# A gated recurrence with a soft mixture of experts: chunks of four units, one exponential for two units, and engine orders written out as lists

## The chip, the cores and the metric

The kernel runs on one core of one Trainium2 chip. The metric is the time on the device in microseconds, as the median of several runs. TensorE is called PE, VectorE DVE, ScalarE ACT, GpSimd POOL, and SyncE, whose queue issues the loads and stores, SP.

## The reference, cut to what matters

x, r_gate and i_gate are 4 x 5056 x 256 (batch, time, channels), in fp32; the output is 20224 x 256.

```
log_a   = 8 * sigmoid(r_gate) * log(clip(sigmoid(a_param)))
a_t     = exp(log_a);  norm = sqrt(max(1 - a_t*a_t, 1e-6))
h       = a_t * h + norm * sigmoid(i_gate) * x     # over time, for each batch
x       = h of all steps, as 20224 rows            # the y of the names below
logits  = x @ phi                                  # 32 slots
d       = softmax of logits over all 20224 rows
slot_in = d.T @ x                                  # 32 x 256, 4 slots for each of 8 experts
out_e   = max(slot_in[e] @ w1[e], 0) @ w2[e]       # 256 -> 1024 -> 256
output  = (softmax of logits over the 32 slots) @ out
```

The softmax over all rows ties the whole input together: no output row is known before the last step of the recurrence is done.

## The kernel before, in words

**Tiles.** The rows are cut into 40 blocks q of 512 (the last has 256). Two blocks make a unit p: unit 0 is q 0, units 1 to 19 are pairs, and unit 20 is q 39. The recurrence runs along the free dimension with channels on the partitions, in two halves h of 128 channels, so everything that comes in with rows on the partitions is transposed by PE.

**Steps of a unit, by their names.** A number behind a name is q, or p.h, or the group.
- Dr, Di, Dx: SP loads r, i and x, 512 KB each.
- TR (line 605): PE transposes r into a "pair" of PSUM banks. SR (616): ACT writes tanh(r/2) from there into slot A.
- EX (680): ACT takes the exponential of A in place, with a scale and a bias per channel; this is a_t. Before, each unit and half has its own.
- SQ (667): POOL squares A into slot N. RT (697): ACT takes the square root of 1 - N for both halves in one instruction.
- SI (629 sigmoid, 631 tanh): ACT makes the input gate for both blocks of a unit at once. A string IV says how, one letter for a unit: S is a sigmoid; P is a tanh with a step of POOL behind it (642); E is a tanh whose 1 is put right by PE, which transposes both i*x and x into the same bank.
- U (651): POOL multiplies gate and x. TU (716): PE transposes the product into a pair. ST (733): DVE multiplies it by the norm. SC (750): DVE scans it and overwrites A with the states.
- TY (774) and YC (790 on DVE, 788 on ACT): the states go back to rows on partitions, through a PSUM bank into a y tile "yn". Either engine can copy.
- For a group g of four blocks: LG (830) logits, LE (843) their running maximum, LD and TE the difference and its transpose, ES (884) and DM (891) two exponentials on ACT, AC (904) the sum over rows on PE, AE (920) its accumulation on DVE.
- CT (1270), CM (1281), CS (1284), CE (1287), RR (1291 to 1293), CN, CH, CL: the softmax over the slots.

Behind the last scan come a short chain (MT, MX, MR, MC, WJ, WE, W, SP), the experts' matmuls L1.0 to L1.7 (1153) and L2.0 to L2.7 (1201) with the weights w1 and w2 (named w10 to w17 and w20 to w27), and the output: HP (1335), HE (1346), OT (1358), OE (1370 on ACT, 1372 on DVE), and OD, the store (1382).

**Chunks.** ACT holds one set of function tables at a time: exp with tanh, sigmoid with tanh, or sqrt. A function of another set brings an ACT_TABLE_LOAD. So the units are cut into chunks, and for a chunk ACT does all SR and EX, then all SI, then all RT:

```
CHUNKS = [2, 2, 2, 2, 2, 2, 2, 2, 2, 2, 1]
IV = 'PPEESSSSSSSSSSSSSSSSP'
```

**Slots.** The data of A, N, x and i lie in 16 slots "b" of 8 KB per partition (two halves of eight 16 KB tiles); r lies in 7 tiles "st" of 4 KB, y in 8 tiles "yn". PSUM has three pairs and two single banks; of the pairs, TR may hold two, TU two and TY one. The weights and the output later use the b and st slots.

**Order.** A planner (class Planner, from line 111) builds the program: each step is a task with an assumed duration, its dependences, a priority and the slots that it takes, and `run` (line 153) starts on each engine the ready task of the best priority, as a list scheduler does. The order in which the tasks start becomes the fixed order of each engine's instructions. SP's loads stand in one queue, each of which waits for its slot, with all behind it. While PE would be idle early on, fillers (1030) keep it at work.

Of the kernel before, what the change touches and what calls it, by code (L numbers as in the profile page):

```python
# [17 lines left out]
J = 4  # L18
# [4 lines left out]
CHUNKS = [2, 2, 2, 2, 2, 2, 2, 2, 2, 2, 1]  # L23
# [5 lines left out]
IV = 'PPEESSSSSSSSSSSSSSSSP'  # L29
# [34 lines left out]
LATE = False  # L64
# [59 lines left out]
class Planner:  # L124
    def __init__(self, slots):
        self.tasks = []
        self.slots = {t: list(range(n)) for t, n in slots.items()}
        self.act_seq = []

        self.pair_max = {}  # L130
        self.pairs_of = {}

        self.pair_left = -1

        self.warm, self.warm_from, self.warm_to = None, 0.0, 0.0
# [14 lines left out]
    def run(self):  # L150
# [11 lines left out]
        self.table = "exp" if GATES0 else "ln"  # L162
# [55 lines left out]
        while n_done < len(self.tasks):  # L218
# [17 lines left out]
            while again:  # L236
                again = False
                for e in ("DVE", "ACT", "PE", "POOL", "SP"):
# [42 lines left out]
    def tag_for(self, b, taken={}):  # L281
        for g in b.tags:
            if b.kept is not None:
                return g
            if b.late is not None and not b.late(self, g):
# [7 lines left out]
        return None  # L293

# [74 lines left out]
def kernel(  # L369
# [122 lines left out]
    def e_const():  # L492
        nc.scalar.preload_act_table_set("exp_and_others" if GATES0 else "natural_log_exp_and_others")
# [8 lines left out]
    t_const = add("POOL", "const", 2.0, prio=-100, emit=e_const)  # L502
# [31 lines left out]
    def load(nm, q):  # L534
# [19 lines left out]
        ld[(nm, q)] = add("SP", f"D{nm}{q}", SPR * n / J + (1.2 if (nm, q) == ("x", PHI) else 0), prio=q, emit=emit, alloc=[] if own else [b], uses=[b] if own else [])  # L554
# [40 lines left out]
    def mk_sr(q):  # L595
# [15 lines left out]
        tr = add("PE", f"TR{q}", 0.25 * n, deps=[ld[("r", q)], t_const], prio=q - TRP, emit=e_tr,  # L611
                 alloc=[rp], uses=[st[("r", q)]], shape="T")

        def e_sr():
            dst = t(A[p])[:, :, i * QT : i * QT + c]
            nc.scalar.activation(dst, t(rp)[:, :, :c], AF.Tanh, scale=0.5)  # L616
# [57 lines left out]
    def mk_exh(p, h):  # L674
# [3 lines left out]
        def e_ex(h=h):  # L678
            v = T["b2"][A[p].slot[0] // 2][:, h::2, :] if len(us) == 2 else t(A[p])[:, h, :c]
            nc.scalar.activation(  # L680
                v, v, AF.Exp, scale=ca[:, h : h + 1], bias=ca[:, h : h + 1]
            )

        EX[(p, h)] = add("ACT", f"EX{p}.{h}", 0.29 + 0.853 * c / 1024 * len(us),
# [3 lines left out]
    def mk_rt(p):  # L688
        c = plen(p)
        wide = p in WIDE  # L690
        for h in range(1 if wide else H):
# [7 lines left out]
            RT[(p, h)] = add("ACT", f"RT{p}.{h}", 0.11 + 0.835 * c / 1024 * (H if wide else 1),  # L699
# [59 lines left out]
    def mk_y(q):  # L759
# [3 lines left out]
        for b0 in range(0, qlen(q) // P, step):  # L763
# [16 lines left out]
            ty = add("PE", f"TY{q}.{b0}", 0.24 * nb, deps=[SC[(p, h)] for h in range(H)],  # L780
# [21 lines left out]

    def exp_phase(pl):
        if pl.act_at >= len(pl.act_seq):
            return True
        return pl.table == "exp" and pl.act_seq[pl.act_at].kind == "exp"

    def mk_group(g):
# [63 lines left out]
        def e_te():  # L872
            for b in range(nb):
# [12 lines left out]
        ES[g] = add("ACT", f"ES{g}", 0.07 + 0.43 * nb * rows / QT, deps=[te], prio=pos - 30, emit=e_es,  # L886
# [38 lines left out]
        AE[g] = add("DVE", f"AE{g}", 0.42, deps=[ac] + ([DM[g], AE[g - 1]] if g else []), prio=pos - 30 + fin,  # L925
# [8 lines left out]
    def e_sa():  # L934
        if GATES0:
# [41 lines left out]
    for k in range(NC):  # L977
# [13 lines left out]
        if not k and not GATES0:  # L991
# [41 lines left out]
    planner.warm, planner.warm_from, planner.warm_to = e_warm, 4.0, WARMT  # L1033
# [10 lines left out]
    def late(pl, tag):  # L1044

        if tag == "st":
            return st[("i", NQ - 1)].tag is not None and len(pl.slots["st"]) >= 2
        return len(pl.slots["b"]) > sum(b.tag is None for b in [*A.values(), *Nb.values(), *xb.values(), *(ib[p] for p in ib if two_i(p)), *lSb, hz] if b.kept is None)
# [24 lines left out]
    sT.late = lambda pl, tag: yn[NQ - 1].tag is not None  # L1073
# [164 lines left out]

    planner.warm_late = lambda pl: LATE and SC[(NP - 1, 0)].start is not None and t_bd[0].start is None


    def quiet(pl):

        return SC[(NP - 3, H - 1)].start is None or l1s[0].start is not None

    def early(pl):
        return SC[(NP - 4, H - 1)].start is None or l1s[0].start is not None

    def late_hl(pl):
        return YC[NQ - 1][-1].end is not None and pl.now >= YC[NQ - 1][-1].end  # L1250
# [3 lines left out]
    def mk_c(g, first):  # L1254
# [7 lines left out]
        hl.late = lambda pl, tag: tag == "yn" and late_hl(pl) or tag != "yn" and l1s[-1].start is not None  # L1262
# [9 lines left out]
        k = add("PE", f"CT{g}", 0.12 * nb, deps=[LE[g]], prio=pc, gate=early, emit=e_ct, alloc=[cp], uses=[lSb[g // 4]], shape="T")  # L1272
# [13 lines left out]
        e = add("ACT", f"CE{g}", 0.12 + 0.43 * nb * rows / QT, deps=[k], prio=pr, kind="exp", gate=lambda pl: pl.act_at >= len(pl.act_seq),  # L1286
# [8 lines left out]
        r = add("DVE", f"RR{g}", 0.7 + 0.5 * nb * rows / QT, deps=[e], prio=pr + 0.2, emit=e_rr, gate=quiet, uses=[lSb[g // 4]])  # L1295
# [4 lines left out]
        k = add("POOL", f"CN{g}", 0.15 + 1.1 * nb * rows / QT, deps=[r], prio=pr, uses=[lSb[g // 4]],  # L1300
# [6 lines left out]
        k = add("POOL", f"CL{g}", 1.0, deps=[k], prio=pr, uses=[hl, lSb[g // 4]],  # L1307
# [9 lines left out]
    for i, g in enumerate(corder):  # L1317
# [6 lines left out]
        for og in ogs:  # L1324
            og.late = lambda pl, tag: l1s[-1].start is not None
        done = {j: [] for j in range(n)}
        for a0 in range(0, m, 8):
# [12 lines left out]
            k = add("PE", f"HP{g}.{a0}", 0.11 * aw / 2, deps=[t_hl], prio=pr - 6, gate=lambda pl: l1s[-1].start is not None,  # L1340
                    emit=e_hp, alloc=[ht], uses=[hl], shape="T")

            def e_he(aw=aw, ht=ht, hT=hT):
# [3 lines left out]
                else:  # L1347
                    nc.vector.tensor_copy(out=dst, in_=v)  # L1348

            he = add(("DVE", "ACT"), f"HE{g}.{a0}", 0.1 + 0.55 * aw / 8, deps=[k], prio=pr - 5, emit=e_he,  # L1350
                     alloc=[hT], uses=[ht], alt={"ACT": 0.1 + 0.45 * aw / 8})
            for b in range(0, aw, 2):
# [14 lines left out]
                def e_oe(b0=b0, op=op, og=ogs[j]):  # L1367
# [3 lines left out]
                    else:  # L1371
# [4 lines left out]
                         uses=[op] + ([] if b0 == 0 else [ogs[j]]), alt={"ACT": 0.5})  # L1376
# [13 lines left out]
    with tc.manual_schedule():  # L1390
        for task in planner.run():
# [29 lines left out]
```

## Time and profile before

| | |
|---|---|
| median of 3 runs | 311.11 us (307.73, 311.11, 313.51) |
| span of the profiled execution | 312.3 us; no other time of this execution is given |
| PE, DVE, ACT, POOL busy | 265.4, 256.6, 253.1, 204.4 us |
| bytes moved | 100.02 MB, 320 GB/s over the span |
| ACT table loads | 32, of 1283 ns each |

A profiled execution has only its span, from the first to the last instruction; it lies 1.2 us above the median of the runs and within them. In the profile's rows, "x36 | 43.9, 1239 | 0.6" means 36 instructions, 43.9 us busy, 1239 ns each on average, and 0.6 us of idle time of the engine just before them. Rows of the order of time begin with the start and the length in us; where rows are merged (x2), the length is that of all of them.

### The profile page before, as it was taken

To read this page: it belongs to the slowest core of one execution; us is meant where nothing else is said; L and a number is where in the kernel's file an instruction comes from. 1 tells how busy PE (TensorE), PEld (TensorE's weight loads), DVE (VectorE), ACT (ScalarE), POOL (GpSimd) and SP (SyncE) were. 2 spreads that over 40 slices of the span, in tenths; PEclk is the share of its full clock that TensorE was granted. 3 is DMA by queue.
4 is the path that set the end of the run, shared out by engine and by line. 5 is a ranking of instruction groups with operands and counts; after the bars stand their busy time and mean duration, and the time that the engine had idled before them with its cause. 6 is when DMAs were issued, how large, how long until landed. Compare 5 with 4: busy or idle time off the path is not lost.

```text
span 312.3 us, 5800 instructions
## 1 busy us (share of the span) xinstructions
PE 265.4 (85%) x2171; PEld 202.4 (65%) x2171; DVE 256.6 (82%) x320; ACT 253.1 (81%) x265; POOL 204.4 (65%) x151
## 2 busy tenths in 40 slices
PE   3998779799796997897977978959998999999880
PEld 2997778575663955855646667555564578888660
DVE  0127878999999899999999999989987648999860
ACT  6599999999999999999999999998550028898560
POOL 4099988988969889789797986895024800347200
PEclk9999799989999798999999979989999999999996
DMA  6997999995957949949569599758979608999997
GB/s 233 416 408 271 413 409 409 394 387 211 416 216 291 418 128 404 352 165 391 209 248 415 203 401 407 251 202 322 319 234 391 219 2 355 400 406 407 403 408 281
DMA packets 30287, 100.02 MB, mean 320 GB/s; under 512 B 3378, under 2 KB 3380, under 8 KB 30260
## 3 DMA queue, kind: packets, MB, share of 16 engines
q1 hardware_dynamic: 30256, 99.66, 82.9%
q8 instruction: 17, 0.28, 0.3%
q14 instruction: 10, 0.08, 0.1%
q10 hardware_dynamic: 4, 0.00, 0.0%
HBM read 78.94 MB, written 20.71 MB: 319 GB/s over the span
## 4 chain that ended last, share of the span: by engine, by line
DVE 30%; PE 27%; ACT 23%; issue 10%; DMA 4%; POOL 3%; SPq 0%; DVEq 0%; POOLq 0%; ACTq 0%
DVE b L750 13%; DVE pair L733 8%; PE bank L1358 5%; ACT b L616 4%; ACT b L680 4%; ACT b L697 4%; PE one L774 3%; PE pair L716 3%; PE bank L1201 2%; PE one L1358 2%; ACT b L629 2%; DMA st<-in_r_gate_dram 2%; POOL b L651 2%; DMA out_dram<-st 2%; DVE yn L790 2%
## 5 line engine op out<-in xcount | busy, mean ns | idle before, releaser
L667 POOL TENSOR_TENSOR b<-b 128x1024 f32<-128x1024 f32 (+1 forms) x40 | 72.8, 1831 | 33.2 <-ACT b L680 32.1
L651 POOL TENSOR_TENSOR b<-b,b 128x1024 f32<-128x1024 f32 x34 | 79.8, 2375 | 3.1 <-ACT b L629 3.1
L750 DVE TENSOR_TENSOR_SCAN b<-b,b,pair 128x1024 f32<-128x1024 f32 (+4 forms) x34 | 68.3, 2012 | 0.5
L733 DVE SCALAR_TENSOR_TENSOR pair<-b,pair 128x1024 f32<-128x1024 f32 (+2 forms) x42 | 48.6, 1156 | 9.1 <-PE pair L716 5.9
L716 PE MATMUL pair<-ident,b 128*128 128x128 f32 x348 | 48.5, 287 | 3.2 <-DVE b L750 2.3
L605 PE MATMUL pair<-ident,st 128*128 128x128 f32 x316 | 45.4, 290 | 6.6 <-DMA st<-in_r_gate_dram 2.6
L716 PEld LDWEIGHTS pair<-ident,b 128*128 128x128 f32 x348 | 41.1, 148 | 13.6 <-issue 5.5
L680 ACT ACTIVATE b<-b,ca 128x1024 f32<-128x1024 f32 (+2 forms) x42 | 49.0, 1187 | 0.6
L605 PEld LDWEIGHTS pair<-ident,st 128*128 128x128 f32 x316 | 37.2, 148 | 16.4 <-DVE b L750 7.6
L616 ACT ACTIVATE b<-pair 128x1024 f32<-128x1024 f32 (+1 forms) x40 | 40.1, 1009 | 6.4 <-PE pair L605 6.0
L774 PE MATMUL one<-ident,b 128*128 128x128 f32 x236 | 38.5, 301 | 6.2 <-DVE yn L790 4.8
L774 PEld LDWEIGHTS one<-ident,b 128*128 128x128 f32 x236 | 29.3, 153 | 12.5 <-DVE yn L790 7.3
L790 DVE COPY yn<-one 128x512 f32<-128x512 f32 x53 | 34.9, 683 | 2.7 <-PE one L774 2.7
L697 ACT ACTIVATE b<-b 128x2048 f32<-128x2048 f32 (+2 forms) x19 | 33.2, 1794 | 0.1
L1358 PE MATMUL bank<-bd,hT 128*128 128x512 f32 x118 | 31.4, 400 | 0.9 <-DVE hT L1348 0.9
L629 ACT ACTIVATE b<-b 128x2048 f32<-128x2048 f32 x16 | 29.7, 1905 | 0.1
L1301 POOL TENSOR_TENSOR b<-b,rs_all 128x512 f32<-128x512 f32 (+2 forms) x11 | 10.6, 963 | 26.8 <-DVE rs_all L1293 22.3
L750 DVE TENSOR_TENSOR_SCAN b<-b,pair 128x1024 f32<-128x1024 f32 (+4 forms) x14 | 25.3, 1806 | 0.2
L774 PE MATMUL pair<-ident,b 128*128 128x128 f32 x72 | 13.1, 312 | 14.1 <-DVE b L750 13.0
L1358 PEld LDWEIGHTS bank<-bd,hT 128*128 128x128 f32 x118 | 21.4, 188 | 5.3 <-DVE hT L1348 1.2
L1346 ACT CAST hT<-bank 128x512 fp32r<-128x512 f32 x13 | 7.7, 592 | 20.4 <-PE bank L1335 20.3
L830 PE MATMUL one<-b,phi_sb 128*32 128x512 f32 (+1 forms) x164 | 23.8, 587 | 0.3 <-DVE b L1284 0.2
(142 smaller groups left out, 420.3 us busy)
## 6 DMA issues: line engine op xcount, KB each, us to landing
b<-in_x_dram SPq DMA_DIRECT2D x39, 512.0 KB, 7.6
st<-in_r_gate_dram SPq DMA_DIRECT2D x38, 512.0 KB, 10.1
b<-in_i_gate_dram SPq DMA_DIRECT2D x38, 512.0 KB, 7.1
out_dram<-st SPq DMA_DIRECT2D x36, 512.0 KB, 5.7
b<-in_moe_w_dram SPq DMA_DIRECT2D x24, 512.0 KB, 5.9
st<-in_moe_w_dram SPq DMA_DIRECT2D x8, 512.0 KB, 8.4
out_dram<-b SPq DMA_DIRECT2D x2, 512.0 KB, 5.5
st<-in_r_gate_dram SPq DMA_DIRECT2D x3, 256.0 KB, 2.8
```

Of the source, the lines that this page charges most:

```text
L605: nc.tensor.transpose(out=o[:, m, :], in_=raw("r", q)[:, m * D + h * P : m * D + (h + 1) * P], identity=ident,)
L616: nc.scalar.activation(dst, t(rp)[:, :, :c], AF.Tanh, scale=0.5)
L651: eng.tensor_tensor(out=o, in0=a, in1=b, op=ALU.mult)
L667: eng.tensor_tensor(out=t(Nb[p])[:, h, :c], in0=v, in1=v, op=ALU.mult)
L680: nc.scalar.activation(v, v, AF.Exp, scale=ca[:, h : h + 1], bias=ca[:, h : h + 1])
L697: nc.scalar.activation(v, v, AF.Sqrt, bias=quarter if f != 1.0 else f, scale=-f)
L716: nc.tensor.matmul(o[:, m, :], raw(nm, q)[:, m * D + h * P : m * D + (h + 1) * P], ident, is_transpose=True, start=(nm == nms[0] and m == ...
L733: nc.vector.scalar_tensor_tensor(v, t(Nb[p])[:, h, :c], 0.5e-3 if gate_of(quads(p)[0]) == "E" else 1e-3, v, op0=ALU.max, op1=ALU.mult)
L750: nc.vector.tensor_tensor_scan(dst, dst, flat()[:, s0:s1], init, op0=ALU.mult, op1=ALU.add)
L774: nc.tensor.transpose(out=flat()[:, b * D + h * P : b * D + (h + 1) * P], in_=t(A[p])[:, h, o : o + P], identity=ident,)
L790: nc.vector.tensor_copy(out=dst, in_=v)
L1358: nc.tensor.matmul(t(op), t(hT)[:, b * P // 2 : (b + 2) * P // 2], T["bd"][part].rearrange("p i d -> p (i d)"), start=(part == 0), stop=(p ...
```

## The change: what it does

- CHUNKS becomes [2, 4, 4, 4, 4, 2, 1].
- EX2: the A of two neighbouring full units of a chunk share one 16 KB tile, and one exponential for each half covers both units (128x2x1024). The input gates were paired already.
- IV: units 2 to 5 instead of 2 and 3 are gated with E.
- The slots: 20 of 8 KB instead of 16, 5 st instead of 7, 6 yn instead of 8. The scratch for dynamic DMA is set to 1024.
- The order: `run_fixed` takes the tasks of each engine from five lists in ORDER. In them 32 instead of 10 copies YC are on ACT, and 54 instead of 47 copies OE.
- CT and what follows it stand ahead of the experts for groups 0 to 2, and behind them for the others (four stood ahead before).
- Fillers may stand from 2.4 us of the plan instead of 4.0. The remaining edits change assumed durations, which a fixed order doesn't use to choose.

The core of the diff:

```diff
-CHUNKS = [2, 2, 2, 2, 2, 2, 2, 2, 2, 2, 1]
+CHUNKS = [2, 4, 4, 4, 4, 2, 1]
-IV = 'PPEESSSSSSSSSSSSSSSSP'
+IV = 'PPEEEESSSSSSSSSSSSSSP'
-N_ST = 7
-N_B = 16
-N_YN = 8
+N_ST = 5
+N_B = 20
+N_YN = 6
-EX2 = False
+EX2 = True
+ORDER = {
...
+    "ACT": """
+        SA LN SR0 SI0 EX0.1 SR1 EX0.0 SR2 SR3 EX1.0 EX1.1 SI1 SR5 RT0.0 RT1.0 SR6 SR4 SI3 EX2.0 SR7 EX2.1 SR9 SI5 SR8 SR10 EX4.0 RT2.0 RT3.0 EX4.1
...
+    def run_fixed(self, orders):
...
+                    if at[e] < len(seqs[e]):
+                        t = seqs[e][at[e]]
+                        if need[id(t)] == 0 and can(t):
+                            begin(t, e)
...
-    planner.warm, planner.warm_from, planner.warm_to = e_warm, 4.0, WARMT
+    planner.warm, planner.warm_from, planner.warm_to = e_warm, 2.4, WARMT
...
-        for task in planner.run():
+        for task in planner.run() if ORDER is None else planner.run_fixed(ORDER):
...
-    nc = _bacc.Bacc("TRN2", target_bir_lowering=False, num_devices=1)
+    nc = _bacc.Bacc("TRN2", target_bir_lowering=False, num_devices=1, dynamic_dma_scratch_size=1024)
```

Three places of the new orders. The lines have new numbers: TR 788, SR 799, SI 812 (sigmoid), EX 866, RT 881, TU 900, ST 917, SC 934, TY 958, YC 972 (ACT) and 974 (DVE), LG 1009, LE 1022, ES 1063, DM 1070, AE 1099. b, st, yn and eS are slots in SBUF, pair and one PSUM banks.

ACT before, from the last exponentials of a chunk of two units (10 and 11) to the next chunk's first tanh:

```order
L680 ACTIVATE b_70<-b_70,ca 128x1024 x2
L629 ACT_TABLE_LOAD
L629 ACTIVATE b_75<-b_75 128x2048
L629 ACTIVATE b_74<-b_74 128x2048
L697 ACT_TABLE_LOAD
L697 ACTIVATE b_74<-b_74 128x2048
L697 ACTIVATE b_71<-b_71 128x2048
L616 ACT_TABLE_LOAD
L616 ACTIVATE b_75<-pair_94 128x2x512
```

And now, in the chunk of the units 10 to 13:

```order
L866 ACTIVATE b_72<-b_72,ca 128x2x1024 x2
L972 COPY yn_77<-one_86 128x2x256
L1070 ACTIVATE dm<-M 128x1
L1063 ACTIVATE eS_85<-one_87 128x512
L812 ACT_TABLE_LOAD
L812 ACTIVATE b_67<-b_67 128x2048
L812 ACTIVATE b_69<-b_69 128x2048 x2
L812 ACTIVATE b_70<-b_70 128x2048
L881 ACT_TABLE_LOAD
L881 ACTIVATE b_73<-b_73 128x2048 x2
L972 COPY yn_77<-one_87 128x2x256
```

The two exponentials serve two units each, four gates and four roots stand behind one load each, and copies of y stand between them.

PE before, where the tanh of a chunk (their TR is line 605) stand among the TU and LG of the chunk ahead:

```order
L605 MATMUL pair_95<-ident,st_64 128x128 x8
L716 MATMUL pair_93<-ident,b_69 128x128 x8
L605 MATMUL pair_94<-ident,st_67 128x128 x8
L716 MATMUL pair_95<-ident,b_75 128x128 x8
L874 MATMUL one_89<-ident,lD_85 128x128 x4
L830 MATMUL one_88<-b_71,phi_sb 32x512
```

And now, at the turn from chunk 3 to chunk 4 (TU11.0, LG4, TU11.1, TR28, TY19.0, TR29, TR30, TU12.0):

```order
L900 MATMUL pair_92<-ident,b_75 128x128 x8
L1009 MATMUL one_86<-b_71,phi_sb 32x512 x3
L1009 MATMUL one_86<-b_74,phi_sb 32x512
L1009 MATMUL one_86<-b_71,phi_sb 32x512 x3
L1009 MATMUL one_86<-b_74,phi_sb 32x512
L900 MATMUL pair_93<-ident,b_75 128x128 x8
L788 MATMUL pair_91<-ident,st_65 128x128 x8
L958 MATMUL one_87<-ident,b_74 128x128 x4
L788 MATMUL pair_92<-ident,st_61 128x128 x8
L788 MATMUL pair_91<-ident,st_64 128x128 x8
L900 MATMUL pair_92<-ident,b_68 128x128 x8
```

The second transpose of r of chunk 4 stands behind a whole LG group, which reads unit 10's states (b_74), and behind two TU; the two after it stand ahead of the next TU.

DVE before, from the first multiply of unit 19 to unit 20:

```order
L733 SCALAR_TENSOR_TENSOR pair_93<-b_75,pair_93 128x1024
L843 TENSOR_SCALAR b_72,M<-one_88,M 128x512
L750 SCALAR_TENSOR_TENSOR b_72<-b_72,b_68,pair_93 128x1024
L733 SCALAR_TENSOR_TENSOR pair_95<-b_75,pair_95 128x1024
L750 SCALAR_TENSOR_TENSOR b_72<-b_72,b_68,pair_95 128x1024
L920 SCALAR_TENSOR_TENSOR accS<-accS,dm,one_89 128x257
L842 COPY M<-M 32x1 x2
L843 TENSOR_SCALAR b_72,M<-one_88,M 64x512
L733 SCALAR_TENSOR_TENSOR pair_93<-b_74,pair_93 128x256
L863 TENSOR_SCALAR lD_85<-one_88,M 64x512
L750 SCALAR_TENSOR_TENSOR b_69<-b_69,b_72,pair_93 128x256
```

And now:

```order
L917 SCALAR_TENSOR_TENSOR pair_93<-b_72,pair_93 128x1024
L1022 TENSOR_SCALAR b_73,M<-one_87,M 128x512
L934 SCALAR_TENSOR_TENSOR b_69<-b_69,pair_93 128x1024
L917 SCALAR_TENSOR_TENSOR pair_91<-b_72,pair_91 128x1024
L934 SCALAR_TENSOR_TENSOR b_69<-b_69,pair_91 128x1024
L917 SCALAR_TENSOR_TENSOR pair_92<-b_75,pair_92 128x256
L917 SCALAR_TENSOR_TENSOR pair_93<-b_75,pair_93 128x256
L934 SCALAR_TENSOR_TENSOR b_66<-b_66,b_69,pair_92 128x256
L934 SCALAR_TENSOR_TENSOR b_66<-b_66,b_69,pair_93 128x256
L1021 COPY M<-M 32x1 x2
L1022 TENSOR_SCALAR b_73,M<-one_86,M 64x512
```

Both show unit 19 (b_75, then b_72 as N) and unit 20. The LE of group 9 (64x512) and its LD stood ahead of the last scan and now stand behind it, as does one AE.

SP's new list puts almost all weights (14 of 16) behind the last inputs, in the order w23 w24 w10 w27 w21 w14 w12 w16 w20 w11 w15 w17 w22 w26; before, all 16 stood there, the w1 first, in the order of their use.

More of the change, by code (lines that the diff above doesn't have):

```diff
@@ L81 @@
+COLD = 8.5
+EX2 = True
 MI = True
-SPR = 1.30
+SPR = 1.29
+SPL = 5.0
 KIND = {
@@ L293, in tag_for, with open, allowed @@
         return None
+    def open(self, gate):
+        what, *of = gate
+        if what == "started":
+            return of[0].start is not None
+        if what == "exp":
+            head = self.act_seq[self.act_at] if self.act_at < len(self.act_seq) else None
+            return head is None or self.table == "exp" and head.kind == "exp"
+        if what == "gates_done":
+            return self.act_at >= len(self.act_seq)
+        assert what == "unless"
+        return of[0].start is None or of[1].start is not None
+    def allowed(self, late, tag):
+        what, *of = late
+        n = len(self.slots[tag])
+        if what == "spare":
+            return n > of[0]
+        if what == "behind":
+            return n > min(J, sum(b.tag is None for b in of[0]))
+        if what == "weights":
+            if tag == "st":
+                return of[0].tag is not None and n >= 2
+            return n > sum(b.tag is None and b.kept is None for b in of[1])
+        if what == "placed":
+            return of[0].tag is not None
+        if what == "ended":
+            if tag == "yn":
+                return of[0].end is not None and self.now >= of[0].end
+            return of[1].start is not None
+        assert what == "begun"
+        return of[0].start is not None
     def twin(self):
@@ L582 @@
     yn = {q: Buf("yn", f"yn{q}") for q in range(NQ)}
-    def yn_late(q):
-        return lambda pl, tag: len(pl.slots["yn"]) > min(J, sum(yn[b].tag is None for b in range(q)))
     for q in range(NQ):
-        yn[q].late = yn_late(q)
+        yn[q].late = ("behind", [yn[b] for b in range(q)])
     SR, SI, U, EX, SQ, RT, ST, SC, YC = {}, {}, {}, {}, {}, {}, {}, {}, {}
@@ L1042, in wpart @@
         return T["st"][b.slot[i]] if b.tag == "st" else T[b.tag][b.slot[0]][:, i, :]
[L1044 to L1048, printed above, removed]
     hz = Buf("b", "hTz")
+    late = ("weights", st[("i", NQ - 1)],
+            [*A.values(), *Nb.values(), *xb.values(), *(ib[p] for p in ib if two_i(p)), *lSb, hz])
     for nm, e in [("w1", e) for e in range(E)] + [("w2", e) for e in range(E)]:
@@ L1237 @@
                 emit=lambda part=part, i=i: e_b(part, i)) for part in range(2) for i in range(2)]
[L1239 to L1250, printed above, removed]
+    quiet = ("unless", SC[(NP - 3, H - 1)], l1s[0])
+    early = ("unless", SC[(NP - 4, H - 1)], l1s[0])
     HL = {}
```

236 lines of the change are left out of this document (188 added, 48 removed).

## The prediction

> **What bounds the kernel now.** I read the page's totals first, then a table of windows cut where the work changes, then ACT's groups and its order of time, then DVE's groups, the waits and SP's issues. The totals single out no engine:
>
> ```profile
> span 312.3 us, 5800 instructions
> PE 265.4 (85%) x2171; PEld 202.4 (65%) x2171; DVE 256.6 (82%) x320; ACT 253.1 (81%) x265; POOL 204.4 (65%) x151
> ```
>
> The windows do. The cuts are the end of the second square root (23.59), the end of unit 19's root (208.37), the end of the last scan (229.87), the first L1 matmul (about 237.5), the last L2 matmul (253.0) and the first output DMA (257.7). The columns are PE, PEld, DVE, ACT, POOL (busy, count), TensorE's granted clock, DMA share and GB/s.
>
> ```profile
> core 0: us, PE busy (x) PEld busy (x) DVE busy (x) ACT busy (x) POOL busy (x), PEclk, DMA share, GB/s
> 0.00:23.59 23.59, 18.57 (x129) 17.47 (x130) 3.93 (x6) 16.81 (x16) 11.57 (x38) 1.00 0.91 353
> 23.59:208.37 184.78, 154.85 (x1287) 117.69 (x1286) 174.14 (x175) 182.13 (x148) 158.82 (x82) 0.95 0.82 319
> 208.37:229.87 21.50, 20.53 (x178) 13.36 (x178) 19.76 (x24) 14.82 (x26) 9.13 (x9) 0.94 0.80 278
> 229.87:237.50 7.63, 6.65 (x67) 4.34 (x65) 4.48 (x17) 1.79 (x5) 1.30 (x3) 1.00 0.98 343
> 237.50:253.00 15.50, 15.33 (x261) 8.50 (x257) 9.54 (x21) 0.00 (x0) 9.51 (x8) 1.00 0.61 225
> 257.70:312.30 54.60, 44.79 (x233) 36.76 (x231) 41.54 (x77) 35.54 (x68) 14.12 (x14) 0.95 0.96 380
> ```
>
> In the 184.78 us of the second window ACT stands still for 2.65 us and DVE for 10.6 us: two engines are full at once. The third window is DVE's backlog, 19.76 of 21.50. The last is the output's DMA at 0.96. So ACT sets 184.8 us, with DVE close behind, and work moved from one of the two to the other buys only the difference.
>
> **ACT's cost per step.** The groups of ACT in the second window (the 128x512 exponential is from the whole run), then one chunk of two units in order of time:
>
> ```profile
> L680 ACT ACTIVATE b<-b,ca 128x1024 f32<-128x1024 f32 x36 | 43.9, 1239 | 0.6
> L616 ACT ACT_TABLE_LOAD x10 | 12.8, 1283 | 0.2
> L697 ACT ACT_TABLE_LOAD x9 | 11.5, 1283 | 0.2
> L629 ACT ACT_TABLE_LOAD x8 | 10.3, 1283 | 0.1
> ...
> L680 ACT ACTIVATE b<-b,ca 128x512 f32<-128x512 f32 x2 | 1.6, 809 | 0.0
> ```
>
> ```profile
> 154.42 2.38 ACT L680 ACTIVATE b<-b,ca 128x1024 f32<-128x1024 f32 x2
> 156.82 1.28 ACT L629 ACT_TABLE_LOAD   x1
> 158.11 3.71 ACT L629 ACTIVATE b<-b 128x2048 f32<-128x2048 f32 x2
> 161.84 1.28 ACT L697 ACT_TABLE_LOAD   x1
> 163.14 3.72 ACT L697 ACTIVATE b<-b 128x2048 f32<-128x2048 f32 x2
> 166.88 1.28 ACT L616 ACT_TABLE_LOAD   x1
> 168.17 1.02 ACT L616 ACTIVATE b<-pair 128x1024 f32<-128x1024 f32 x1
> ...
> 220.74 1.05 ACT L788 COPY yn<-one 128x512 f32<-128x512 f32 x2
> ```
>
> From end to start a table switch takes 1.30 us (161.84 to 163.14), a 128x2048 gate or root 1.86, a tanh about 0.98, and a copy of y, in a pair of 1.05, about 0.48 behind another.
>
> **The terms, ACT, from the second root to unit 19's root.**
> - Table loads: 26 stand in that stretch before (9+8+9), 20 after, counted in the new order. 6 x 1.30 = -7.8.
> - Exponentials: 36 become 18 of twice the size, which the trace doesn't show. Two cost 2.38. From 512 to 1024 elements the time grows by 1239-809 = 0.43, so 2048 should take 1.24+0.86 = 2.10: 18 x 0.28 = -5.0. The ends are 0 (nothing saved) and -8.6 (the 1.905 of other 128x2048 instructions); I take 2.10, which has this instruction's own slope.
> - Copies of y: 18 move into the stretch, 18 x 0.48 = +8.6.
> - Two tanh are now ahead of the second root (-2.0); the last tanh (0.60), an eS, a dm and the 0.095 of two more roots with the quarter come in (+1.5): -0.5.
>
> The sum is -4.7, so unit 19's root ends at 203.7. Unit 20's root then needs two loads, two small exponentials, nine copies, one gate, CE0, an eS and itself, 2.6+1.05+4.3+0.6+0.5+0.5+0.6 = 10.2: 213.9. Unit 20's two multiplies and scans close it. Before they ran from 227.04 to 229.87 with an LD of 0.66 between; without it 2.2, so **the last scan ends no earlier than 216.1 by ACT**.
>
> A page of the Trainium skill weighs against my 1.30: "ScalarE: Activation LUTs", section "What ACT_TABLE_LOAD costs", puts a switch at 1283 ns for the load and about 1380 ns of drain behind it. By it the six loads would be worth 16 us. The trace agrees with 1283 ns, but the sigmoid starts 1.29 us after the load's start, so no drain shows here.
>
> **The terms, DVE.** Its groups up to the last scan, two copies back to back, and the last scan:
>
> ```profile
> L750 DVE TENSOR_TENSOR_SCAN b<-b,b,pair 128x1024 f32<-128x1024 f32 x26 | 60.8, 2341 | 0.3
> L733 DVE SCALAR_TENSOR_TENSOR pair<-b,pair 128x1024 f32<-128x1024 f32 x38 | 46.4, 1220 | 7.5 <-PE pair L716 4.4 <-ACT b L616 1.3 <-ACT b L697 1.0
> L790 DVE COPY yn<-one 128x512 f32<-128x512 f32 x53 | 34.9, 683 | 2.7 <-PE one L774 2.7
> ```
>
> ```profile
> 188.20 1.28 DVE L790 COPY yn<-one 128x512 f32<-128x512 f32 x2
> ...
> 229.12 0.75 DVE L750 TENSOR_TENSOR_SCAN b<-b,b,pair 128x256 f32<-128x256 f32 x1
> ```
>
> A copy behind another takes 0.60, a multiply then 1.16, a scan 2.25 (about 0.09 overlap). Before the last scan there are 47 copies instead of 67 (-12.0), one max and subtract pair less (-1.2), one square less (-0.7); one LE with its two small copies, one LD and one AE now come behind the scan (-2.0): DVE has 16 us less to do.
>
> But a chunk of four makes DVE wait once. Unit 6's first multiply needs unit 6's root, and from 23.6 ACT has first 14 tanh, 8 double exponentials, 8 gates, 5 roots, 7 loads and three small ones, 13.7+16.2+14.9+9.5+9.1+1.2 = 64.6: with 1 us of idle, 89.2. From there DVE has 28 multiplies, 28 scans (two of them cut), unit 20's pair of each, 27 copies, 7 LE, 6 AE and two max and subtract pairs: 33.2+64.8+16.2+4.7+2.3+2.4 = 123.6. With 3 us of small waits, of the 10.6 above, **the last scan ends at 215.8 by DVE**. Both sums meet at 216.
>
> Two engines that are both full and wait for one another lose more than either sum. What speaks of it are the waits at the turn of a chunk:
>
> ```profile
> ACT b L616 <- PE pair L605: 6.0, 4, 2.3
> PEld pair L605 <- DVE b L750: 7.6, 11, 1.0
> PEld one L774 <- DVE yn L790: 7.3, 13, 2.4
> ```
>
> I add 3 us, between 0 and the 7.6 of the second row once more: **219** against 229.87. Behind the last scan stand now LE9, RR0 and LD9 ahead of or between what the end waits for (some 2.5 us of DVE work, two copies less), partly beside LG10: 7.6 becomes 8.6. The L1 and L2 matmuls are the same 256: 15.5. The output stays bound by its DMA: 4.7+54.6; CM, CS and CT of one more group (1.2 us of DVE, four transposes) lie beside it. 219+8.6+15.5+59.3 = 302.4, that is 9.9 less than the profiled 312.3. The median of the three runs is 1.2 lower, 311.1, so I say **301 us**.
>
> Costed at nothing: the two more units gated by tanh, with 32 more transposes (some 4 us of PE, which has 30 us to spare in the second window; without that cover the first scans of chunk 1 are 4 us later, and ACT still sets the root of unit 6); fillers from 2.4 us on; the smaller scratch (the trace shows no price; what it could hurt is SP's issue); the start, where x of unit 0 is the tenth tile instead of the sixth, beside the gates that ACT then does first (bounds -3 to +3).
>
> **Weights.** SP issues them in order of time like this:
>
> ```profile
> 185.78 11.85 SPq L1058 DMA_DIRECT2D st<-in_moe_w_dram  x6
> 199.99 18.52 SPq L1058 DMA_DIRECT2D b<-in_moe_w_dram  x10
> 219.00 15.51 SPq L1060 DMA_DIRECT2D b<-in_moe_w_dram  x14
> 235.34 3.09 SPq L1060 DMA_DIRECT2D st<-in_moe_w_dram  x2
> ```
>
> They end at 238.4, some 13 us before the last is used. After, 26 of the 32 transfers are w24's and those behind it, and w24 waits for unit 17's second multiply, which by the DVE sum comes 111.5 of the 123.6 us in, at 203. At 1.11 us each, the pace of the third row, they are issued by 232, while L1 begins at 227.6 and its last users come some 10 us later: hidden. At 1.85, the second row, w11, which the second L1 step needs, comes at 236, 8 us late, and the last at 251. I take 0, since the third row is the pace at which nothing but the transfers holds SP.
>
> **Rivals.**
> 1. Slower: the tanh get tied to the scans. PE's order puts transposes of r behind LG and TU that wait for a scan or for the pair it frees, so ACT waits for DVE at four turns of a chunk (into chunks 2, 3, 4 and 5), and DVE, which then lacks roots, falls behind as well. For it speak the first two rows of waits; against it that ACT had only 2.65 us of idle. With w us per turn it costs 4w: the gain is gone at 2.5, 2% slower begins at about 4, and where ACT waits for one unit's multiplies and scans (6.8) it is 27 us less 10, or 328. Chance 0.10.
> 2. No change: the copies on ACT stall it. Each needs a PE transpose that itself needs a scan, and six y tiles instead of eight hold these back (third row). 18 copies at 0.5 us of wait are 9 us: 310. Chance 0.13.
> 3. The weights come late, for 5 us, midway between these two: 306. Chance 0.15.
> 4. Better: no loss between the engines, and a better start, -3-3: 295. Chance 0.13.
> 5. The page's drain is there after all, unseen by rows: -8.3 for six loads, 293. Chance 0.02, since no row of this trace shows it.
>
> **How the numbers follow.** The forecast, 301 with 298 to 304, has 0.47. The range of 293 to 310 takes in rivals 2 to 5 and the ends of the exponential's cost, and leaves out rival 1 and the edges of 2. Faster by over 2% is below 304.9, and 2% is about what a measurement of this kernel tells from no change: the forecast, rivals 4 and 5 and a quarter of 3 make 0.66; within 2%, rival 2 and the rest of 3, 0.24; slower, rival 1, 0.10.
>
> **What would show it.** Right: 26 table loads instead of 32; exponentials of 128x2x1024 near 2.1 us; the end of unit 19's root near 204, of the last scan near 219, the first output DMA near 247; DVE idle for some us ahead of unit 6's first multiply, and full from there. Wrong: ACT idle ahead of tanh at the turn of a chunk (rival 1) or ahead of copies (2); an L1 or L2 matmul released by a DMA (3); a last window other than 54 to 56 us.

## The result, and the profile after

The changed kernel takes **300.6 us** in the median (300.04, 300.17, 301.02, 302.21), where the kernel before takes 310.88 on the same chip. The ratio is 0.971 (95% interval 0.964 to 0.978). Measured a second time (after_again below), it was 300.95 against 312.37, 0.964 (0.958 to 0.969). Three executions lay far above all others of their kernel (426.77 us of split_exp, 329.93 of lists_two, 624.59 of the kernel before), and the medians and ratios leave them out.

The page's totals of the changed kernel, to be held against the first fence of the prediction:

```profile
span 298.3 us, 5854 instructions
PE 259.9 (87%) x2223; PEld 198.9 (67%) x2223; DVE 232.3 (78%) x289; ACT 251.2 (84%) x271; POOL 204.5 (69%) x150
```

DVE has 24 us less to do (256.6 before), 14.5 of them copies of y (45.9 us before, 31.4 now). ACT has only 2 less. The windows, cut at the same events as before (second root, unit 19's root, last scan, first L1, last L2, first output DMA):

```profile
core 0: us, PE busy (x) PEld busy (x) DVE busy (x) ACT busy (x) POOL busy (x), PEclk, DMA share, GB/s
0.00:22.77 22.77, 19.56 (x151) 18.80 (x151) 4.60 (x7) 18.39 (x18) 13.63 (x38) 1.00 0.92 352
22.77:201.66 178.89, 154.66 (x1372) 116.89 (x1369) 164.65 (x157) 175.71 (x144) 160.17 (x82) 0.99 0.88 337
201.66:213.96 12.30, 11.56 (x100) 7.00 (x100) 11.85 (x11) 12.07 (x20) 5.56 (x7) 1.00 1.00 370
213.96:223.62 9.66, 8.27 (x75) 5.63 (x76) 6.85 (x22) 4.16 (x12) 2.90 (x4) 1.00 0.98 381
223.62:238.79 15.17, 15.17 (x261) 9.21 (x262) 4.98 (x13) 0.00 (x0) 5.00 (x5) 1.00 0.47 177
243.61:298.30 54.69, 45.84 (x237) 36.94 (x235) 35.02 (x73) 38.92 (x76) 16.35 (x16) 0.97 0.96 380
```

Unit 19's root ends 5.9 us sooner counted from the second root (178.89 instead of 184.78). The backlog behind it, DVE's before, shrank from 21.50 to 12.30, and now ACT is full in it too. The chain from the last scan to L1 grew from 7.5 to 9.66; the rest is as it was. The profiled execution's time is 300.04, its span 298.3.

Three rows of the changed kernel carry the terms. The first is ACT's doubled exponential. The other two are the stretch from the first multiply of unit 6 to the last scan, and DVE's largest wait from 87 us on:

```profile
L866 ACT ACTIVATE b<-b,ca 128x2048 f32<-128x2048 f32 x18 | 37.5, 2098 | 0.2
```

```profile
87.38:213.96 126.58, 109.54 (x969) 77.45 (x967) 123.86 (x115) 123.83 (x116) 107.37 (x59) 0.99 0.84 318
```

```profile
DVE pair L917 <- ACT b L881: 2.5, 3, 1.4
```

DVE works 123.86 us of 126.58 there, and ACT 123.83: two engines side by side, each with under 3 us of idle time. Of the 2.5 us of waits for roots, 1.4 stand just ahead of the stretch, before unit 6's first multiply.

### The profile page after: what moved, and what is told of

Same layout as the page of the kernel before. It is cut to its first block, busy times and chain, and to the rows that moved or that the text cites. A ratio compares the mean times of both kernels' runs of the same rounds, so it can differ in the third digit from the quotient of the medians.

```text
span 298.3 us, 5854 instructions
## 1 busy us (share of the span) xinstructions
PE 259.9 (87%) x2223; PEld 198.9 (67%) x2223; DVE 232.3 (78%) x289; ACT 251.2 (84%) x271; POOL 204.5 (69%) x150
## 4 chain that ended last, share of the span: by engine, by line
PE 35%; ACT 24%; DVE 14%; DMA 11%; POOL 6%; issue 6%; SPq 0%; ACTq 0%; POOLq 0%; DVEq 0%
DVE b L934 7%; PE bank L1526 7%; DMA b<-in_i_gate_dram 6%; PE pair L788 5%; ACT b L881 4%; DVE pair L917 4%; PE pair L900 4%; POOL b L834 4%; ACT b L812 3%; DMA st<-in_moe_w_dram 3%; ACT b L799 3%; ACT b L866 3%; PE one L1526 3%; ACT L881 3%; POOL b L850 2%
## 5 line engine op out<-in xcount | busy, mean ns | idle before, releaser
L850 POOL TENSOR_TENSOR b<-b 128x1024 f32<-128x1024 f32 (+2 forms) x41 | 73.6, 1816 | 9.0 <-ACT b L866 4.7
L900 PE MATMUL pair<-ident,b 128*128 128x128 f32 x380 | 49.4, 278 | 7.3 <-DVE b L934 3.0
L934 DVE TENSOR_TENSOR_SCAN b<-b,pair 128x1024 f32<-128x1024 f32 (+6 forms) x26 | 47.6, 1848 | 0.2
L934 DVE TENSOR_TENSOR_SCAN b<-b,b,pair 128x1024 f32<-128x1024 f32 (+2 forms) x22 | 45.4, 2073 | 0.4
L866 ACT ACTIVATE b<-b,ca 128x2048 f32<-128x2048 f32 (+3 forms) x24 | 42.7, 1795 | 0.2
L958 PE MATMUL one<-ident,b 128*128 128x128 f32 x208 | 31.6, 281 | 7.2 <-DVE yn L974 2.5
L958 PEld LDWEIGHTS one<-ident,b 128*128 128x128 f32 x208 | 22.6, 141 | 17.3 <-DVE yn L974 6.6
L1538 ACT COPY st<-bank 128x512 f32<-128x512 f32 x33 | 18.8, 603 | 6.9 <-PE bank L1526 4.5
L974 DVE COPY yn<-one 128x512 f32<-128x512 f32 x32 | 21.2, 682 | 2.2 <-PE one L958 2.1
L1009 PE MATMUL one<-b,phi_sb 128*32 128x512 f32 x152 | 21.3, 618 | 0.0
```

The costliest lines, as they stand in the source:

```text
L850: eng.tensor_tensor(out=t(Nb[p])[:, h, :c], in0=v, in1=v, op=ALU.mult)
L866: nc.scalar.activation(v, v, AF.Exp, scale=ca[:, h : h + 1], bias=ca[:, h : h + 1])
L900: nc.tensor.matmul(o[:, m, :], raw(nm, q)[:, m * D + h * P : m * D + (h + 1) * P], ident, is_transpose=True, start=(nm == nms[0] and m == ...
L934: nc.vector.tensor_tensor_scan(dst, dst, flat()[:, s0:s1], init, op0=ALU.mult, op1=ALU.add)
L958: nc.tensor.transpose(out=flat()[:, b * D + h * P : b * D + (h + 1) * P], in_=t(A[p])[:, h, o : o + P], identity=ident,)
```

## The experiments

Times are medians; "before" is the old kernel on the same chip. split_exp, six_loads, copies_dve and no_lists ran on one chip; after_again, lists_two, lists_two_ex2 and relisted on a second; the others on a third. The old kernel's median lies between 311.81 and 312.71 on them, so less than 1 us between runs of different chips says little. In the text, differences from the change are taken from the 300.95 of after_again. The last five columns are one profiled execution: end of the last scan, first L1, end of the last L2, first output DMA, and the span.

| run | us | before | ratio (95%) | scan | L1 | L2 end | output | span |
|---|---|---|---|---|---|---|---|---|
| before | 311.1 | | | 229.87 | 237.36 | 252.98 | 257.76 | 312.3 |
| the change | 300.6 | 310.88 | 0.971 (0.964 to 0.978) | 213.96 | 223.62 | 238.79 | 243.61 | 298.3 |
| after_again | 300.95 | 312.37 | 0.964 (0.958 to 0.969) | 214.38 | 224.04 | 239.21 | 244.03 | 298.7 |
| split_exp | 304.4 | 311.81 | 0.977 (0.972 to 0.982) | 219.27 | 228.93 | 244.10 | 248.92 | 303.6 |
| six_loads | 311.17 | 311.81 | 0.998 (0.995 to 1.002) | 224.02 | 233.68 | 248.85 | 253.67 | 308.4 |
| copies_dve | 313.21 | 311.81 | 1.004 (1.000 to 1.007) | 227.21 | 236.86 | 252.03 | 256.85 | 312.4 |
| no_lists | 345.55 | 311.81 | 1.106 (1.099 to 1.113) | 258.40 | 267.25 | 282.57 | 287.42 | 343.8 |
| lists_two | 311.29 | 312.37 | 0.997 (0.994 to 1.001) | 219.55 | 231.71 | 248.94 | 253.87 | 309.5 |
| lists_two_b | 308.43 | 312.71 | 0.989 (0.983 to 0.995) | 219.28 | 229.71 | 245.35 | 250.62 | 306.2 |
| two_split | 309.81 | 312.71 | 0.992 (0.989 to 0.995) | 224.17 | 232.65 | 248.17 | 253.02 | 308.3 |
| lists_two_ex2 | 303.73 | 312.37 | 0.972 (0.966 to 0.979) | 217.75 | 225.95 | 241.48 | 246.33 | 301.8 |
| relisted | 304.84 | 312.37 | 0.977 (0.970 to 0.984) | 214.74 | 227.72 | 242.88 | 247.87 | 303.4 |
| relisted_hz | 303.17 | 312.71 | 0.973 (0.967 to 0.980) | 214.29 | 224.22 | 239.38 | 244.37 | 300.8 |
| relisted_b | 302.06 | 312.71 | 0.970 (0.963 to 0.978) | 213.64 | 223.09 | 240.62 | 245.51 | 300.7 |

### Is ACT's work on the path? Each term put back alone

**split_exp.** The tile of two units stays, only the instruction is cut in two:

```diff
-                nc.scalar.activation(v, v, AF.Exp, scale=ca[:, h : h + 1], bias=ca[:, h : h + 1])
+                for w in ([v[:, 0], v[:, 1]] if len(us) == 2 else [v]):
+                    nc.scalar.activation(w, w, AF.Exp, scale=ca[:, h : h + 1], bias=ca[:, h : h + 1])
```

> The changed kernel with each of the 18 doubled exponentials issued as two of 1024 again; slots, lists and order stay. By the trace a pair of the old kernel took 2.38 us and a doubled one takes 2.10, so ACT gets 18 x 0.28 = 5.0 us more, 8 of the 18 ahead of unit 6's root (2.2). Theory (ACT and DVE are both full up to the last scan): unit 19's root ends 5 us later and the last scan 2.2 to 5, so 303 to 306 us, against 300.6. Rival (only DVE bounds now, ACT has slack that takes it up): within 1 us of 300.6.

It took 304.4, within the theory's range. Its 36 exponentials last 1242 ns each. Unit 19's root, ACT's row below, ends at 206.97 instead of 201.66, and the last scan is later by the same 5.31:

```profile
205.06 1.91 ACT L882 ACTIVATE b<-b 128x2048 f32<-128x2048 f32 x1
```

So ACT has no slack that could take up 5 us. DVE's waits from 87 us on show how the delay reaches it, first of the changed kernel, then of this one:

```profile
DVE pair L917 <- ACT b L881: 2.5, 3, 1.4
DVE pair L917 <- PE pair L900: 0.8, 3, 0.3
```

```profile
DVE pair L918 <- ACT b L882: 4.0, 3, 1.8
DVE pair L918 <- PE pair L901: 2.0, 4, 0.8
```

Unit 6's first multiply begins 1.78 later (89.16), and behind it DVE waits longer for roots and for the transposes of the product (the rows for roots include the wait just ahead of that multiply, 1.4 and 1.8). The profiled execution took 305.39, the two others 304.31 and 304.38, so the 5.31 is at the upper end: by the medians the split costs 3.5.

**six_loads.**

```diff
+            if q in (17, 21, 29):
+                nc.scalar.activation(tiny, quarter, AF.Sqrt)
             if how == "S":
                 nc.scalar.activation(v, v, AF.Sigmoid)
```

> The changed kernel with a square root of 128x1 into an unused tile ahead of one sigmoid in each of the chunks of units 6 to 9, 10 to 13 and 14 to 17: three switches to the root's table and back, six loads, as many as the change took out of the stretch. Theory (a switch costs 1.30 and ACT bounds): 6 x 1.30 + 3 x 0.2 = 8.4 us more on ACT, 2.8 of it ahead of unit 6's root, so 306 to 309 us. If a drain of 1.38 us stood behind each load unseen, 8 us more: 314 to 317. Rival (ACT has slack): 303.4 or less, the 2.8 ahead of unit 6 alone.

311.17: more than expected, 10.2 above the change, nearly all of the gain. ACT in order of time, at one of the three places:

```profile
80.45 1.28 ACT L813 ACT_TABLE_LOAD   x1
81.74 0.20 ACT L813 ACTIVATE tiny<-quarter 128x1 f32<-128x1 f32 x1
81.96 1.28 ACT L815 ACT_TABLE_LOAD   x1
83.26 1.91 ACT L815 ACTIVATE b<-b 128x2048 f32<-128x2048 f32 x1
```

From 80.45 to 83.26 are 2.81 us, 8.4 for three places. A function starts 1.29 to 1.30 us behind the start of its load, with nothing between, and the second load starts 0.02 behind the end of the root: no drain on either side, and the time is far from 314 to 317. Unit 19's root ends 10.06 later than in the changed kernel, and DVE's wait for roots from 87 us on is 9.9 us instead of 2.5:

```profile
209.81 1.91 ACT L884 ACTIVATE b<-b 128x2048 f32<-128x2048 f32 x1
```

```profile
DVE pair L920 <- ACT b L884: 9.9, 4, 4.3
```

Of the 10.06, 8.4 are the inserted instructions. The other 1.7 are waits of ACT, under an order that was made without them: up to that root it waits 2.9 us for transposes of r instead of 2.2, 0.8 for a load of the input gate, where it had no such wait, and 0.5 for an earlier instruction of its own.

**copies_dve.** In the lists, 18 names YC move from ACT to DVE, from YC10.0 to YC31.0. A piece of ACT's list:

```diff
-RT6.0 RT9.0 RT7.0 YC10.0 YC10.2 RT8.0 SR19
+RT6.0 RT9.0 RT7.0 RT8.0 SR19
```

> The changed kernel with the 18 copies of y that stand on ACT between the root of unit 6 and that of unit 19 put back on DVE, each at the place of DVE's list where it was due: DVE gets 18 x 0.60 = 10.8 us more, ACT 18 x 0.48 = 8.6 less. Theory (DVE is full from unit 6's first multiply): its last scan is 8 to 11 us later, 308 to 311 us; the copies are what makes room for the loads' and exponentials' gain. Rival (ACT alone sets the time): 301 us or less.

313.21, 12.3 above the change and beyond the theory's 8 to 11; the rival is out. DVE, from 87.38 to its last scan, stands idle for only 5.1 us and has 10.9 us more work than in the changed kernel (123.86):

```profile
87.38:227.21 139.83, 116.02 (x973) 81.19 (x971) 134.75 (x133) 117.05 (x99) 107.81 (x60) 0.94 0.80 302
```

ACT, with 8.6 us less to do, ends unit 19's root not earlier but 10.4 later (212.05). The reason stands in ACT's waits up to the last scan, first of the changed kernel, then of this one:

```profile
ACT b L799 <- PE pair L788: 2.2, 3, 1.5
```

```profile
ACT b L799 <- PE pair L788: 12.1, 7, 4.8
ACT dm L1070 <- DVE b L1022: 4.3, 2, 4.0
```

The tanh wait for PE's transposes of r. These stand in PE's fixed order behind work that waits for DVE. PE's waits between 85 us and the last scan, for scans and for y tiles that DVE copies, show it; the changed kernel has 1.4 and 2.5 us of the two:

```profile
PE pair L900 <- DVE b L934: 6.0, 4, 2.2
PE one L958 <- DVE yn L974: 5.6, 6, 1.9
```

This is the first rival's mechanism, and here it came as soon as DVE was late. An order searched for these copies on DVE was not tried, so how much of the 12.3 us lies in the order stays open.

### Are the lists only a carrier?

**no_lists.** Everything but the lists is the change:

```diff
-ORDER = {
...
-}
+ORDER = None
```

> The changed kernel without the five lists: chunks of four, doubled exponentials, 20 slots and the gates as in the change, but the tasks ordered by the planner's priorities, as before. Theory (fewer loads and doubled exponentials bring the gain, whatever orders them): 300 to 306 us. Rival (longer chunks are only worth it with an order made for them; by priorities tanh wait for the pairs that scans free, as in my first rival, and DVE lacks roots at the turns): 315 us or more, by the price of a turn in that rival up to 328.

345.55, 44.6 above the change and 11% slower than before. The waits of ACT (23 to 260 us) and of DVE (the whole run):

```profile
ACT b L739 <- PE pair L728: 26.8, 15, 5.2
ACT dm L1010 <- DVE b L962: 20.7, 6, 6.3
```

```profile
DVE pair L857 <- ACT b L821: 30.4, 4, 18.3
DVE pair L857 <- PE pair L840: 13.9, 10, 2.2
```

ACT waits 26.8 us for transposes of r, DVE then 30.4 for roots, once 18.3 at a stretch. Long chunks under the planner's priorities are the first rival in full, and dearer than the 328 that it was priced at. My theory here, that the gain comes whatever orders the tasks, is refuted.

**lists_two, lists_two_b, lists_two_ex2, two_split.** These have chunks of two and lists from a search. two_split keeps the lists of lists_two_ex2; the others have their own:

```diff
-CHUNKS = [2, 4, 4, 4, 4, 2, 1]
+CHUNKS = [2, 2, 2, 2, 2, 2, 2, 2, 2, 2, 1]
-IV = 'PPEEEESSSSSSSSSSSSSSP'
+IV = 'PPEESSSSSSSSSSSSSSSSP'
 # lists_two and lists_two_b besides: EX2 = False, N_ST, N_B, N_YN = 7, 16, 8
 # two_split: lists_two_ex2 with the edit of split_exp
```

> Chunks of two units, single exponentials, the slots and gates of before, but the engines' orders written out as lists that a search made for just this kernel. The difference to before is the lists (and four small settings that came with the change: fillers from 2.4 us, groups 0 to 2 ahead, scratch). Theory (lists are worth much in themselves, as no_lists made it seem, 45 us): 301 to 305 us. Rival (priorities were good enough for chunks of two; lists are needed only to make the longer chunks work): 307 to 311 us.

> lists_two with its lists searched again, now such that the short DVE instructions of the chain behind the last scan (the copy of the maximum, W, and CH) don't run beside a POOL instruction. In lists_two W took 1.74 us there instead of 0.29, and L1 began 12.2 us behind the last scan, against 9.7 in the changed kernel. Theory (the lists alone bring the last scan 10 us forward, and most of it was lost behind it): 306 to 309 us. Rival (the stage behind the scan waits for the weights, whose slots come free late with 16 slots): 310 to 312 us again.

> Chunks of two units with doubled exponentials, 20 slots and the lists of a search for just this: the change without its longer chunks and without the gates of units 4 and 5. It has the six loads again. Theory (the loads are worth 8 to 10 us, as six_loads showed): 308 to 311 us. Rival (longer chunks give back at the start what they save in loads, since DVE waits until unit 6's root at 87 us and has to do everything behind it): within 3 us of the change, 300 to 304 us.

> lists_two_ex2 with each of its 18 doubled exponentials issued as two of 1024: chunks of two, 20 slots and the lists stay. Theory (ACT bounds there too): 18 x 0.28 = 5.0 us more, so 308 to 309 us; the doubled exponentials are then about half of what separates it from before, and the rest is slots and lists. Rival (slots and lists do it, and ACT has slack): 304 to 305 us.

lists_two, 311.29, looks like its rival. But its last scan ends 10 us before that of the old kernel, and the chain behind it took 12.2 us; my lists had put POOL's work beside it, and a scale of DVE (W) took 1.74 there instead of 0.27. Searched again with such neighbours forbidden, lists_two_b takes 308.43, as its theory said: **the lists, with the small settings that came with them, bring some 4 us**. Its last weight is issued only at 231.3, behind the start of L1, but PE waits for no weight there, so its rival is out. The doubled exponentials are worth 309.81 - 303.73 = **6.1 us** with chunks of two under lists made for them, a little more than the theory's 5.0; against lists_two_b, whose lists were made for single ones and which has 16 slots, it is 4.7. lists_two_ex2, without the longer chunks and the gates of units 4 and 5, is only **2.8 us** from the change: its rival was right, not my theory.

How can six loads cost 10 us when put in, and the chunks that save them bring 2.8? DVE answers. The windows of lists_two_ex2, up to where unit 6 starts in the changed kernel and from there to its last scan:

```profile
22.77:87.38 64.61, 54.29 (x467) 42.82 (x468) 57.22 (x56) 64.32 (x47) 56.51 (x29) 1.00 1.02 400
87.38:217.75 130.37, 110.23 (x984) 77.45 (x983) 129.55 (x135) 128.45 (x114) 107.78 (x59) 1.00 0.83 308
```

The changed kernel's row for the first of these is

```profile
22.77:87.38 64.61, 56.68 (x504) 46.45 (x502) 52.64 (x52) 63.96 (x47) 58.37 (x31) 1.00 0.97 381
```

With chunks of two DVE does 57.22 us of work by 87.38, with chunks of four 52.64: the longer chunk makes it wait for a root, 4.3 us at once, where it waits 1.2 for roots with chunks of two. To pay for that, 32 copies of y are on ACT instead of 15, 17 x 0.48 = 8.2 us, which is most of the 8 x 1.30 = 10.4 us that 26 loads instead of 34 (groups of 12, 8 and 8 and six single ones) set free. The loads pay for the copies, and the copies for the wait. This is worked out from the sums; no run takes the copies and the loads apart.

### Does a better order exist?

**relisted, relisted_hz, relisted_b.** Only the lists differ: names are moved within them, some copies between ACT and DVE, and in relisted_b two steps from DVE to POOL. For relisted, the end of POOL's list shows it; relisted_hz is one swap more:

```diff
 # relisted, POOL
-P139 LD8 SQ20.0 U39 SQ20.1 SZ HZ CN0 BZ CN1 CL0 CL1
+LD8 P139 SQ20.1 U39 SZ CN2 HZ CN0 CL2 CN1 BZ CL1
 # relisted_hz, POOL
-LD8 P139 SQ20.1 U39 SZ CN2 HZ CN0 CL2 CN1 BZ CL1
+LD8 P139 SQ20.1 U39 SZ HZ CN2 CN0 CL2 CN1 BZ CL1
```

> The changed kernel with its five lists searched further: a few tasks moved on each engine, nothing else. If DVE from unit 6 on and the output's DMA are full, as the trace says, no order brings more than the 2 to 3 us that DVE still waits: 298 to 301 us.

> relisted with one swap in POOL's list: the fill of a 128x2048 tile with zeros, 1.80 us, stands ahead of a CN instead of behind it, so that it lies beside the last scans. In relisted DVE's copy of 1x128 took 1.99 us beside that fill and ended with it (221.45 and 221.38), where the changed kernel has 0.21. Theory (DVE can't run this copy while POOL works): the copy takes 0.2 to 0.4 and the time is 1.6 to 1.8 us less, 303 us. Rival (the copy is slow for its place behind the copy of y): it takes 1.9 again, 304.8 us.

> The changed kernel with its lists searched further, as relisted, but with those short DVE instructions kept out of POOL's way. If this was the whole loss of relisted: 298 to 301 us. If something else holds the stage behind the last scan: 302 to 305 us.

relisted ends its last scan within 1 us of the change, but takes 304.84, outside the expected range: L1 begins 13.0 us behind the scan instead of 9.7. DVE there, then POOL:

```profile
219.46 1.99 DVE L1270 COPY mrep<-mmax 1x128 f32<-1x128 f32 x1
219.64 1.81 DVE L1099 SCALAR_TENSOR_TENSOR accS<-accS,dm,one 128x257 f32<-128x257 f32 x1
```

```profile
218.59 1.05 POOL L1469 TENSOR_TENSOR b<-b,rs_all 128x512 f32<-128x512 f32 x1 [6.16 <-ACT yn L972]
219.58 1.80 POOL L1311 MEMSET b<- 128x2048 f32 x1
```

The copy of 1x128 ends at 221.45, with the fill (221.38), and a matmul that needs it comes 1.88 us after PE's last work. In relisted_hz the fill (HZ) lies beside the scans, and the copy is short:

```profile
213.44 1.80 POOL L1311 MEMSET b<- 128x2048 f32 x1 [1.46 <-PE one L1009]
```

```profile
219.01 0.25 DVE L1270 COPY mrep<-mmax 1x128 f32<-1x128 f32 x1
```

303.17, as the theory said. L1 begins 9.9 us behind the scan again, 3.05 less. The copy's 1.74 are a part of that. The rest are the 28 matmuls behind it, which run at a mean granted clock of 0.66 in relisted and 1.00 in relisted_hz:

```profile
221.82 4.11 PE L1083 MATMUL bank<-yn,eS 128*32 128x257 f32 x28
```

```profile
219.62 2.80 PE L1083 MATMUL bank<-yn,eS 128*32 128x257 f32 x28
```

relisted_b, searched with such neighbours forbidden, starts L1 at 223.09 but ends L2 17.5 us later instead of 15.2. Two of its L1 steps wait for their weights, 1.94 us together:

```profile
226.32 0.64 PE L1330 MATMUL one<-b,yn 128*32 128x256 f32 x8 [1.30 <-DMA b<-in_moe_w_dram]
227.60 1.50 PE L1330 MATMUL one<-b,yn 128*32 128x256 f32 x24 [0.64 <-DMA b<-in_moe_w_dram]
```

This is the prediction's third rival, under another order of the loads. At 302.06 relisted_b doesn't beat the change, so no run here does.

## Why the prediction was right, and where it was wrong

**301 against 300.6 is a hit of the sum, not of all its terms, and in part luck.** Two errors cancel: the span came out 4.1 us below the sum, and the step from span to median, taken with the wrong sign, gave back 2.9 of them. The mechanism was right: ACT and DVE are both full up to the last scan, fewer loads and doubled exponentials relieve ACT, and copies move across.

- *Loads.* 26 remain of 32, and a switch is 1.30: as said. The page "ScalarE: Activation LUTs" of the Trainium skill, section "What ACT_TABLE_LOAD costs", has about 1380 ns of drain behind a load; six_loads puts the next function 1.29 to 1.30 us behind the load's start.
- *Doubled exponentials.* Taken at 2.10 from the old instruction's slope; 2.098 measured. Split again they cost 3.5 us in the changed kernel and 6.1 with chunks of two, around the 5.0 of the term (4.7 against lists_two_b).
- *ACT's sum.* The stretch was to be 180.1 and is 178.89; with a start 0.8 us shorter (within its bounds) unit 19's root ends at 201.66, not 203.7.
- *DVE.* Unit 6's first multiply came at 87.38 (89.2 said), and DVE's work from there at 123.86 (123.6 said).
- *The step that failed* is DVE's waits, taken at 3 us of small ones and 3 more because "two engines that are both full and wait for one another lose more than either sum". DVE lost 2.72 in all. The last scan ended at 213.96 instead of 219: 3.3 us by the waits, 1.8 by the earlier start of unit 6. This is the fourth rival's mechanism, no loss between the engines. copies_dve and six_loads show that the argument isn't wrong in itself: under orders not made for them the engines do lose to one another (up to 1.7 us in six_loads; in copies_dve unit 19's root is 10.4 late although ACT has less to do). The order made for this kernel avoids it, and I gave that order no worth.
- *Behind the scan.* 9.66 instead of 8.6, then 15.17, 4.82 and 54.69 against 15.5, 4.7 and 54.6. The weights were hidden: the last issue ended at 221.5, ahead of L1, earlier than the 232 worked out, and PE is busy 15.17 of 15.17 us.
- *From span to median.* The sum gave a span of 302.4; it is 298.3, 4.1 less. I took the old profile to lie 1.2 us above the median. But times lie about 1.7 us above spans (300.04 to 298.3), so that execution, at a span of 312.3, took about 314 (an estimate) and was 3 above it. This gives back 2.9 of the 4.1, and the median of the change lies 0.6 above its profiled execution. What is left, 0.6, less the rounding of 301.2 to 301, is the miss of 0.4.

Of the rivals, the first (tanh tied to the scans) cost 2.2 us of ACT's waits here and is what no_lists and copies_dve suffer from. The second didn't come: ACT waits for no copy of y ahead of the last scan. The third didn't come in the change, where no L1 or L2 matmul waits for a weight, but relisted_b pays 1.94 us to it. The fifth is ruled out by six_loads.

What the prediction did not see is the order of worth. It took the loads as the largest term and the lists as their carrier. By the runs the way from 312 to 301 is: lists about 3 to 4 (two_split, lists_two_b), doubled exponentials 5 to 6, longer chunks with their gates 3. And without lists the same chunks are some 34 us slower than before. The worth of the slots, of the two gates, of SP's order and of the output's copies by itself was not separated.

## What to carry to other kernels

Where two engines are both full, an instruction saved on one is worth its whole time only if work can follow it across; this is argued here from the sums. So price a saving together with the work that it makes room for, and with the wait that the new structure brings to the other engine. A longer batch between table switches needs an order made for it: under the old scheduler this one looked 11% slower than before. And make a searched order know which instructions disturb each other, because in lists_two and relisted it put a long POOL instruction beside a short DVE one on the critical chain.

## What the hardware showed that I had not expected

**A short DVE copy or scale can last as long as the POOL work beside it.** The copy of 1x128 took 1.99 us beside a POOL fill and 0.25 away from it. In relisted_b a scale of 128x16, elsewhere 0.17, took 3.25 and ended at 227.91 with a row of POOL work that ended at 227.88 (it held up no matmul there):

```profile
224.66 3.25 DVE L1459 TENSOR_SCALAR rs_all<-rs_all 128x16 f32<-128x16 f32 x1
```

```profile
225.15 0.99 POOL L1394 MEMSET bd<- 128x512 f32 x2
226.08 1.80 POOL L1310 MEMSET b<- 128x2048 f32 x1
```

The Trainium skill, "SBUF — State Buffer", section "Who interferes with whom", says that a DVE copy or tensor_scalar in a two-port mode and a GpSimd instruction lock each other out for the whole instruction. The rows agree for the fill, but the scale waited through several POOL instructions, one behind another. Not every copy waits: in the changed kernel two of 32x1 took 0.31 us together beside the same fill (DVE at 213.99, POOL from 212.68 to 214.48).

**PE's granted clock follows PE's idle time, and the old kernel's time goes with it.** In no_lists PE is busy 3.83 of 10 us at clock 0.50, and the clock is back at 1.00 only in the window after the next:

```profile
200.00:210.00 10.00, 3.83 (x16) 1.77 (x16) 7.15 (x4) 8.22 (x6) 10.00 (x5) 0.50 0.73 274
210.00:220.00 10.00, 8.87 (x60) 6.58 (x61) 7.45 (x8) 3.78 (x6) 3.45 (x3) 0.83 0.64 238
220.00:230.00 10.00, 9.99 (x93) 6.17 (x92) 9.93 (x10) 9.77 (x8) 5.68 (x4) 1.00 0.72 252
```

This fits the Trainium skill's "TensorE: Matmul & The Clock Gate", section "What's actually happening", by which idle PE falls to half its clock. A short wait of PE costs more than itself by it: in relisted the 28 matmuls soon after 1.88 us of idle PE took 4.11 us instead of 2.80 (clock 0.66), and in lists_two, soon after 2.52 us of idle PE, the first 48 of L1 took 4.38 instead of the 2.80 of lists_two_b (clock 0.63). Over 18 runs of the kernel before on one chip the span lay between 308.2 and 312.4 us and the mean clock between 0.960 and 0.982; a line through them falls by 1.45 us for each 0.01 of clock (correlation -0.81). The changed kernel had 0.983 to 0.988. Some of its gain may be this clock, but not much: at 0.986 the line gives 307.8 us for the old kernel (an estimate, beyond the clocks measured), against spans of 298.1 to 300.4 for the changed one. Whether fewer waits raise the clock or the clock shortens the waits was not separated.
